# A state-space layer and a gated feed-forward on one core: diagonal matmuls taken out, an inverse root in Newton steps, and the next chunk's input groups moved into the down-projection

## The chip, the cores and the metric

The kernel runs on one core of a Trainium2 chip. TensorE (PE) multiplies matrices into PSUM, VectorE (DVE), ScalarE (ACT) and GpSimd (POOL) work on whole tiles, and SyncE (SP) issues the DMAs. The metric is device time in microseconds (us); lower is better.

## The reference

x is 2048 x 512 in bf16. All matrices are 512 x 512 or, in the feed-forward, 512 x 1376 and 1376 x 512.

```python
xn = _layernorm(x)
dt = exp(log_dt); Lam_bar = exp(dt * Lam); B_bar = ((Lam_bar - 1) / Lam)[:, None] * Bmat
Bu = einsum("bld,pd->blp", xn, B_bar)
h_t = Lam_bar * h_(t-1) + Bu_t                       # over 2048 steps, complex, 512 states
y = 2 * einsum("blp,dp->bld", h, Cmat).real + xn * Dskip
ffn = (silu(xn @ w_gate) * (xn @ w_up)) @ w_down
out = x + y + ffn
```

## The kernel before

The 2048 rows are cut into 4 chunks of 512, each of 4 tiles of 128 rows. Everything stays in SBUF. The complex recurrence is turned by a table of cosines and sines of t times theta into a real scan (decay r), so the steps of a chunk c are:

- **Layer norm.** VectorE takes statistics per tile (L507, L509), adds epsilon (L511, "ve"), GpSimd raises to the power -0.5 (L513, "rstd"). In chunks 0 and 1 VectorE scales (L518); in chunks 2 and 3 it makes a bias (L522, "nmr") and ScalarE scales (L524). The result is xn_sb, which has 8 tile slots.
- **Transpose** of xn into xnT, which has two slots, one for even and one for odd chunks. Chunk 0 uses TensorE (L580) and copies by ScalarE (L586); chunks 1 to 3 use one DMA transpose each (`xt_chunk_dma`, "xTd").
- **FFN groups.** For each of 11 slices of the hidden width one PSUM bank of gate and one of up (L741; chunk 0's first gates in quarters, L768). ScalarE takes silu of the gate (L754, L793, "sg") and copies the up group (L805, "uf", 3 slots); VectorE multiplies them into hT (L807).
- **B groups** ("B c"): 8 PSUM banks of xn times B (L821), copied by ScalarE into u_sb (L828, L830). A copy out of PSUM is called an evacuation below.
- **State steps** on VectorE, for each of 4 slices pt: two products with the tables and a sum (L851, L854, L856: pin1, pin2, v), two scans (L860), two products back (L866, L870: pout1, pout2), a sum into hss (L875), and between chunks some operations on 2 or 4 columns (L873, L882 to L887).
- **Down-projection** `dc_chunk(c)`: "dA" multiplies hT by w_down for 4 tiles (L909, 11 matmuls a tile), "dB" adds hss times the prepared C matrices W12 into the same 4 banks (L925, 8 matmuls a tile). Then VectorE adds the residual while it reads PSUM (L933, L936, "oadd") and a DMA stores the tile.

The term xn * Dskip goes two ways. In chunks 0 and 1 (`rs_dve_from=8`), dA has four more matmuls of 128 x 128 per tile: xnT times diagonal matrices diagD made from Dskip (L912; L498 makes them). In chunks 2 and 3 VectorE multiplies xn by dsk (L596), adds x (L598), and oadd adds that.

W12 needs parameters: cos and sin of theta (L638, L636), then a chain of small products over 128 x 4 (`dve_tt`, L617, and `dve_ts`, L622) to g_re and g_im; then ScalarE scales C (L713, L715) and VectorE finishes (L717, L720). The sine and cosine tables: GpSimd makes t times theta (L692, "tm"), VectorE reduces it into range once for the sine (L694, L696) and once for the cosine (L702, L704), ScalarE takes the sine (L698, L706), GpSimd negates one copy (L700).

**What sets the order.** The kernel records every operation as a task with an engine, a duration that is written by hand (`est`) and what it reads and writes. A planner (`_schedule`) keeps TensorE and SP in the order in which they were recorded. On VectorE, ScalarE and GpSimd it orders the tasks by when they could start and by the longest path behind them. Each engine then runs its list in that order, with semaphore waits, so an instruction that waits holds up all behind it. A DMA transpose waits for all DMAs recorded before it, and a plain DMA waits for the last transpose before it. The order of the program's body before:

```python
        ln_chunk(3)
        dc_chunk(0, mid=lambda: xt_chunk_dma(2))
        u2 = ssm_b_chunk(2)
        ssm_elem_chunk(2, u2)
```

`mid` is called between dA and dB. PSUM has 8 banks; dA holds four until the oadds have read them, and `next_bank` gives the others out in turn.

Of the kernel before, what the change touches and what calls it, by code (L numbers as in the profile page):

```python
# [10 lines left out]
ALU = alu_op_type.AluOpType  # L11
# [13 lines left out]
    rs_dve_from=8,  # L25
# [226 lines left out]
def bass_parallel_sum__ssm_conv_s5__swiglu_ffn__prompt_kernel(  # L252
# [32 lines left out]
    with es:  # L285
# [38 lines left out]
        wtmp = scrC[:, 0:2048].rearrange("p (k d) -> p k d", k=4)  # L324
        vq = sb("vq", [128, NU, 2, 2, CH], B16)
# [8 lines left out]
        praw = sb("praw", [128, 4, PT], B16)  # L334
        prow = sb("prow", [4, 4, 128], B16)
        ecst = sb("ecst", [128, PT], F32)
        diagD = sb("diagD", [128, KT, 128], B16)
# [65 lines left out]
        def dma(name, dst, src, writes, nbytes, reads=(), after=(), out_=False, eng="sp", xpose=False, **kw):  # L403
            after = tuple(after)
            if xpose:
                after = after + tuple(dma_tasks)
                fn = lambda e, dst=dst, src=src: e.dma_start_transpose(out=dst, in_=src)
                est, nb = 2000.0, int(nbytes * 0.8)
            else:
                if xp_state[0] is not None:  # L410
                    after = after + (xp_state[0],)
                fn = lambda e, dst=dst, src=src: e.dma_start(dst, src, **kw)
                est, nb = 330.0 + nbytes / 900.0, nbytes
            t = g.add(eng, fn, reads=reads, writes=writes, name=name, dma=True, after=after, out=out_, est=est, nbytes=nb)
            dma_tasks.append(t)
            if xpose:
                xp_state[0] = t
            return t
# [9 lines left out]
        pload("ld_dskp", 3, A_Dskip)  # L428
# [15 lines left out]

        def loads_stage_b2():
            dma("ld_cre", CT[:, 0], A_C_re, [("CT", 0)], 512 * 512 * 2, xpose=True)
            dma("ld_cim", CT[:, 1], A_C_im, [("CT", 1)], 512 * 512 * 2, xpose=True)
            dma("ld_x8", x_sb[:, 8:12, :], x_v[:, 8:12, :], [("x", a) for a in range(8, 12)], 4 * TILEB)
            dma("ld_wd0", wd[:, 0:FT - 1, :], B_w_down[0:(FT - 1) * 128, :].rearrange("(k p) d -> p k d", p=128), [("wd", 0)], (FT - 1) * 128 * 1024)
            dma("ld_wd1", wd[0:fsz[-1], FT - 1, :], B_w_down[(FT - 1) * 128:Fh, :], [("wd", 1)], fsz[-1] * 1024)  # L450
            dma("ld_x12", x_sb[:, 12:16, :], x_v[:, 12:16, :], [("x", a) for a in range(12, 16)], 4 * TILEB)
            dma("ld_dsk", dsk[:], A_Dskip.partition_broadcast(128), [("dsk",)], 128 * 1024)
# [33 lines left out]
        def params_t(ks):  # L486
            slot = next_tr()

            def tr(e, slot=slot):
                for k in ks:  # L490
                    inst = e.transpose(out=ptr[:, slot, 4 * k:4 * k + 4], in_=prow[0:4, k, :], identity=ident[0:4, 0:4])
                return inst
            g.add("pe", tr, reads=[("prow", k) for k in ks] + [("ident",)], writes=BK(slot), name="parT%d" % ks[0], est=30 * len(ks), ninst=len(ks))
            g.add("dve", lambda e, slot=slot: e.tensor_copy(out=praw[:, ks[0]:ks[-1] + 1].rearrange("p k a -> p (k a)"), in_=ptr[:, slot, 4 * ks[0]:4 * ks[-1] + 4]),
                  reads=BK(slot), writes=[("praw", k) for k in ks], name="parTev%d" % ks[0], est=80, prio=5000.0)
            if 3 in ks:
                for kt in range(KT):
                    g.add("dve", lambda e, kt=kt: e.tensor_scalar(out=diagD[:, kt, :], in0=ident[:], scalar1=praw[:, 3, kt:kt + 1], scalar2=None, op0=ALU.mult),  # L498
                          reads=[("praw", 3), ("ident",)], writes=[("diagD", kt)], name="diagD%d" % kt, est=90)
# [6 lines left out]
        def ln_stats(a, order=False):  # L506
# [9 lines left out]
        def ln_scale(a, norm_act):  # L516
            if not norm_act:
                ln_xn[a] = g.add("dve", lambda e, a=a: e.tensor_scalar(out=xn_sb[:, a % NXN, :], in0=x_sb[:, a, :], scalar1=mv[:, a, 0:1], scalar2=rstd[:, a:a + 1],  # L518
                                                                        op0=ALU.subtract, op1=ALU.mult),
                                  reads=[("x", a), ("mv", a), ("rstd", a)], writes=[("xn", a % NXN)], name="xn%d" % a, est=350)  # L520
            else:
                g.add("dve", lambda e, a=a: e.scalar_tensor_tensor(out=nmr[:, a:a + 1], in0=mv[:, a, 0:1], scalar=-1.0, in1=rstd[:, a:a + 1], op0=ALU.mult, op1=ALU.mult),  # L522
                      reads=[("mv", a), ("rstd", a)], writes=[("nmr", a)], name="nmr%d" % a, est=70)
                g.add("act", lambda e, a=a: e.activation(out=xn_sb[:, a % NXN, :], in_=x_sb[:, a, :], func=AF.Identity, scale=rstd[:, a:a + 1], bias=nmr[:, a:a + 1]),  # L524
                      reads=[("x", a), ("rstd", a), ("nmr", a)], writes=[("xn", a % NXN)], name="xn%d" % a, est=710)

        def ln_tile(a, norm_act):
            ln_stats(a)
            ln_scale(a, norm_act)

        def ln_head():
            for a in range(4):
                ln_stats(a)
            for a in range(4):
                ln_scale(a, False)
            seq = [ln_bn[0], ln_ag[0], ln_ve[0], ln_bn[1], ln_ag[1], ln_xn[0], ln_ve[1], ln_xn[1], ln_bn[2], ln_ag[2], ln_ve[2], ln_bn[3], ln_ag[3], ln_ve[3], ln_xn[2], ln_xn[3]]
            for p, q in zip(seq, seq[1:]):
                if p not in q.deps:
                    q.odeps.add(p)

# [6 lines left out]
        def ln_chunk(c):  # L547
            for a in range(4 * c, 4 * c + 4):
                ln_tile(a, _CFG["ln_norm_act"][c])
# [40 lines left out]
        def xt_chunk_dma(c):  # L590
            s0 = (4 * c) % NXN
            dma("xTd%d" % c, xnT[:, c % 2].rearrange("p j k t -> p (j k) t"), xn_sb[:, s0:s0 + 4, :],
                XNC(c), 4 * TILEB, reads=[("xn", s0 + j) for j in range(4)], xpose=True)

        def resid_tile(a):
            g.add("dve", lambda e, a=a: e.tensor_tensor(out=xn_sb[:, a % NXN, :], in0=xn_sb[:, a % NXN, :], in1=dsk[:], op=ALU.mult),  # L596
                  reads=[("xn", a % NXN), ("dsk",)], writes=[("xn", a % NXN)], name="rs1_%d" % a, est=340)
            g.add("dve", lambda e, a=a: e.tensor_tensor(out=xn_sb[:, a % NXN, :], in0=xn_sb[:, a % NXN, :], in1=x_sb[:, a, :], op=ALU.add),  # L598
                  reads=[("xn", a % NXN), ("x", a)], writes=[("xn", a % NXN)], name="rs2_%d" % a, est=340)
# [15 lines left out]
        def dve_tt(outn, an, bn, op):  # L615
            o, a_, b_ = S(outn), S(an), S(bn)
            small("dve", outn, lambda e: e.tensor_tensor(out=o, in0=a_, in1=b_, op=op), R(an, bn), R(outn))  # L617
# [70 lines left out]
        def _tables():  # L688
            thn = S("thn")
            for pt in range(PT):  # L690
                b = pt % 2
                g.add("pool", lambda e, pt=pt, b=b: e.tensor_scalar(out=tm[:, b, :], in0=iot[:], scalar1=thn[:, pt:pt + 1], scalar2=None, op0=ALU.mult),  # L692
                      reads=R("thn") + [("iot",)], writes=[("tm", b)], name="tm%d" % pt, est=900, prio=_CFG['prio_tab'])
# [6 lines left out]
                g.add("pool", lambda e, pt=pt, b=b: e.tensor_scalar(out=sin2[:, pt, 1, :], in0=sin2[:, pt, 0, :], scalar1=-1.0, scalar2=None, op0=ALU.mult),  # L700
                      reads=[("sinT", pt, 0)], writes=[("sinT", pt, 1)], name="msinT%d" % pt, est=700, prio=_CFG['prio_tab'])
                g.add("dve", lambda e, b=b: e.tensor_scalar(out=tt1[:, b, :], in0=tm[:, b, :], scalar1=0.25, scalar2=MAGIC, op0=ALU.add, op1=ALU.add),  # L702
                      reads=[("tm", b)], writes=[("tt1", b)], name="tt1c%d" % pt, est=400, prio=_CFG['prio_tab'])
                g.add("dve", lambda e, b=b: e.scalar_tensor_tensor(out=tz[:, b, :], in0=tt1[:, b, :], scalar=MAGIC, in1=tm[:, b, :], op0=ALU.subtract, op1=ALU.subtract),  # L704
                      reads=[("tt1", b), ("tm", b)], writes=[("tz", b)], name="tzc%d" % pt, est=660, prio=_CFG['prio_tab'])
                g.add("act", lambda e, pt=pt, b=b: e.activation(out=cosT[:, pt, :], in_=tz[:, b, :], func=AF.Sin, scale=-TWO_PI, bias=halfpi[:, 0:1]),  # L706
                      reads=[("tz", b), ("halfpi",)], writes=[("cosT", pt)], name="cosT%d" % pt, est=700, prio=_CFG['prio_tab'])
# [49 lines left out]
        def ffn_gate_quarters(c, tiles):  # L757
# [21 lines left out]
            params_t([0, 1, 2, 3])  # L779
# [60 lines left out]
        def ssm_elem_chunk(c, units):  # L840
            hb = c % 2
            for (pt, us) in units:
# [16 lines left out]
                for ri in range(2):  # L859
# [3 lines left out]
                        reads=[("v", sl), ("car", c)] + R("r"), writes=[("q", sl, ri)], name="scan%d_%d_%d" % (c, pt, ri), est=1180)  # L863
# [27 lines left out]
        def dc_chunk(c, mid=None, split_last=False):  # L891
# [10 lines left out]
            for (lt, c0, nc_), bk in zip(items, banks):  # L902
                dg = (4 * c + lt < _CFG["rs_dve_from"])
                assert not (dg and nc_ != 512)

                def mmA(e, bk=bk, lt=lt, hb=hb, c=c, c0=c0, nc_=nc_, dg=dg):
# [3 lines left out]
                    if dg:  # L910
                        for kt in range(KT):
                            inst = e.matmul(pbank[:, bk, kt * 128:(kt + 1) * 128], lhsT=xnT[:, c % 2, lt, kt, :], rhs=diagD[:, kt, :], start=False, stop=False)  # L912
                    return inst
                g.add("pe", mmA, reads=[("hT", hb, i) for i in range(FT)] + [("wd", 0), ("wd", 1)] + (XN(c, lt) + [("diagD", kt) for kt in range(KT)] if dg else []),
                      writes=BK(bk), name="mm_dA%d_%d" % (4 * c + lt, c0), est=FT * (216 if nc_ == 512 else 110) + (KT * 60 if dg else 0), ninst=FT + (KT if dg else 0))
            if mid is not None:
                mid()
            for (lt, c0, nc_), bk in zip(items, banks):
# [13 lines left out]
                if a < _CFG["rs_dve_from"]:  # L932
# [111 lines left out]
```

## Time and profile before

| what | value |
|---|---|
| median of 3 runs | 183.66 us (183.64 to 184.3) |
| the profiled execution | 183.74 us |
| its span, first to last instruction | 182.0 us |
| granted TensorE clock in it | 0.999 |
| bytes read and written in HBM | 6.46 MB and 2.10 MB |

The profile comes from one execution. Its table of engines gives the time in which each engine was busy. The chain of work that ended last is followed back from the last instruction: at each step to what released it, or to the instruction before it on its engine; it says which work sets the end. The groups of instructions by line give how many there are, their busy time and the mean duration of one in ns; as instructions overlap a little, the spacing from start to start in the timeline can be shorter. In the groups, after the second bar, stands the idle time of the engine just before them, with what ended it. In the timeline the columns are start, length, engine, line and operation; "SPq" is SyncE's queue that issues DMAs.

### The profile page before, as it was taken

What the parts mean: (1) busy time and instruction counts of PE and PEld (TensorE: products, weight loads), DVE (VectorE), ACT (ScalarE), POOL (GpSimd) and SP (SyncE); (2) the same over time, 40 slices, a digit from 0 to 9 for tenths busy, and PEclk for the clock granted to TensorE, in tenths of its full rate; (3) what the DMA queues carried; (4) which work ended last, traced back from release to release, by engine and by line L of the source; (5) the groups of instructions that cost most, each with busy time, mean ns of one, the idle gap of its engine ahead of it and who ended that gap; (6) DMA issues with size and microseconds to landing.
All of it is one profiled execution on the core that took longest, in us unless ns stands there. A gap on an engine that the chain in (4) does not pass through costs nothing.

```text
span 182.0 us, 2595 instructions
## 1 busy us (share of the span) xinstructions
PE 177.6 (98%) x943; PEld 87.0 (48%) x943; DVE 167.5 (92%) x359; ACT 87.4 (48%) x155; POOL 26.2 (14%) x37
## 2 busy tenths in 40 slices
PE   8899999999999999999999999999999999999994
PEld 3684444444444454444444455444444444444643
DVE  3799889999999998999999999999999999999933
ACT  3249987966798308057766480026667620000000
POOL 3597775000000004000000130000000000000000
PEclk9999999999999999999999999999999999999999
DMA  5993665669400000630000000620000000010202
GB/s 123 318 382 88 117 135 78 120 157 359 131 0 4 0 0 0 122 114 0 0 0 0 0 4 0 115 101 15 0 4 2 0 2 0 0 32 0 86 29 86
DMA packets 23404, 12.39 MB, mean 68 GB/s; under 512 B 15104, under 2 KB 23392, under 8 KB 23392
## 3 DMA queue, kind: packets, MB, share of 16 engines
q1 hardware_dynamic: 23360, 12.23, 25.3%
q8 instruction: 7, 0.11, 0.3%
q14 instruction: 5, 0.04, 0.1%
q10 hardware_dynamic: 32, 0.00, 0.0%
HBM read 6.46 MB, written 2.10 MB: 47 GB/s over the span
## 4 chain that ended last, share of the span: by engine, by line
PE 93%; DVE 3%; DMA 1%; POOL 1%; issue 0%; DVEq 0%
PE pb L741 39%; PE pb L909 21%; PE pb L925 15%; PE pb L821 15%; PE pb L768 1%; DMA x_sb<-in_A_x_dram 1%; DVE st L507 1%; PE pb L912 1%; DVE xn_sb L518 1%; POOL rstd L513 1%; POOL sm L643 1%; DVE mv L509 0%; DVE diagD L498 0%; DVE osb L936 0%; PE pb L580 0%
## 5 line engine op out<-in xcount | busy, mean ns | idle before, releaser
L741 PE MATMUL pb<-xnT,wu 128*128 128x512 bf16 (+1 forms) x176 | 43.7, 379 | 0.0
L909 PE MATMUL pb<-wd,hT 128*128 128x512 bf16 (+3 forms) x187 | 39.7, 367 | 0.0
L860 DVE TENSOR_TENSOR_SCAN vq<-sm,car,vq 128x512 bf16<-128x512 f32 x32 | 39.5, 1269 | 0.1
L741 PE MATMUL pb<-xnT,wg 128*128 128x512 bf16 (+1 forms) x152 | 38.4, 379 | 0.0
L805 ACT ACTIVATE uf<-pb 128x512 bf16<-128x512 f32 (+1 forms) x44 | 26.0, 605 | 16.1 <-DVE hT L807 9.3
L925 PE MATMUL pb<-W,hss 128*128 128x512 bf16 (+1 forms) x136 | 28.3, 366 | 0.0
L821 PE MATMUL pb<-xnT,BT 128*128 128x512 bf16 x128 | 28.1, 379 | 0.0
L741 PEld LDWEIGHTS pb<-xnT,wu 128*128 128x128 bf16 (+1 forms) x176 | 17.6, 100 | 20.1
L909 PEld LDWEIGHTS pb<-wd,hT 128*128 128x128 bf16 (+1 forms) x187 | 18.0, 98 | 18.5
L754 ACT ACTIVATE sg<-pb 128x512 bf16<-128x512 f32 (+1 forms) x38 | 22.6, 606 | 7.1 <-PE pb L741 6.9
L741 PEld LDWEIGHTS pb<-xnT,wg 128*128 128x128 bf16 (+1 forms) x152 | 15.3, 101 | 17.6
L513 POOL TENSOR_TENSOR rstd<-ve,mhalf 128x1 f32<-128x1 f32 x16 | 9.6, 616 | 76.1 <-DVE ve L511 76.1
L925 PEld LDWEIGHTS pb<-W,hss 128*128 128x128 bf16 x136 | 13.2, 98 | 13.9
L821 PEld LDWEIGHTS pb<-xnT,BT 128*128 128x128 bf16 x128 | 12.5, 98 | 15.1
L807 DVE TENSOR_TENSOR hT<-sg,uf 128x512 bf16<-128x512 bf16 (+1 forms) x44 | 18.4, 424 | 1.3 <-ACT uf L805 0.8
L828 ACT ACTIVATE u_sb<-pb 128x512 bf16<-128x512 f32 x16 | 9.5, 596 | 17.2 <-PE pb L821 17.2
L507 DVE BATCH_NORM_STATS2 st<-x_sb 128x6 f32<-128x512 bf16 x16 | 10.2, 683 | 3.0 <-DMA x_sb<-in_A_x_dram 3.0
L830 ACT ACTIVATE u_sb<-pb 128x512 bf16<-128x512 f32 x16 | 9.6, 598 | 3.2 <-PE pb L821 3.2
L866 DVE TENSOR_TENSOR scrA<-vq,cosT 128x1024 bf16<-128x1024 bf16 x16 | 10.9, 684 | 0.0
L870 DVE TENSOR_TENSOR scrA<-vq,sin 128x1024 bf16<-128x1024 bf16 x16 | 10.9, 684 | 0.0
L854 DVE TENSOR_TENSOR scrA<-u_sb,sin 128x1024 bf16<-128x1024 bf16 x16 | 10.9, 682 | 0.0
L851 DVE TENSOR_TENSOR scrA<-u_sb,cosT 128x1024 bf16<-128x1024 bf16 x16 | 10.9, 680 | 0.0
(74 smaller groups left out, 143.2 us busy)
## 6 DMA issues: line engine op xcount, KB each, us to landing
out_dram<-osb SPq DMA_DIRECT2D x15, 128.0 KB, 1.7
x_sb<-in_A_x_dram SPq DMA_DIRECT2D x3, 512.0 KB, 7.5
wd<-in_B_w_down_dram SPq DMA_DIRECT2D x1, 1280.0 KB, 7.1
wg<-in_B_w_gate_dram SPq DMA_DIRECT2D x2, 384.0 KB, 4.6
wu<-in_B_w_up_dram SPq DMA_DIRECT2D x1, 768.0 KB, 6.9
wg<-in_B_w_gate_dram SPq DMA_DIRECT2D x1, 608.0 KB, 7.9
wu<-in_B_w_up_dram SPq DMA_DIRECT2D x1, 608.0 KB, 9.0
x_sb<-in_A_x_dram SPq DMA_DIRECT2D x4, 128.0 KB, 3.0
```

Source lines behind the costliest of these rows:

```text
L507: ln_bn[a] = g.add("dve", lambda e, a=a: e.bn_stats(out=st[:, a, :], in_=x_sb[:, a, :]), reads=[("x", a)], writes=[("st", a)], name="bnst% ...
L513: g.add("pool", lambda e, a=a: e.tensor_tensor(out=rstd[:, a:a + 1], in0=ve[:, a:a + 1], in1=mhalf[:, a:a + 1], op=ALU.pow), reads=[("ve", ...
L741: inst = e.matmul(pbank[0:fs, bk, :].rearrange("p (j t) -> p j t", j=4), lhsT=w[:, kt, i * 128:i * 128 + fs], rhs=xnT[:, c % 2, :, kt, :], ...
L754: g.add("act", lambda e, sl=sl, bk=bk, fs=fs: e.activation(out=sg[0:fs, sl, :], in_=pbank[0:fs, bk, :], func=AF.Silu), reads=BK(bk), write ...
L805: g.add("act", lambda e, ul=ul, bk=bk, fs=fs: e.activation(out=uf[0:fs, ul, :], in_=pbank[0:fs, bk, :], func=AF.Identity), reads=BK(bk), w ...
L807: g.add("dve", lambda e, sl=sl, ul=ul, fs=fs, i=i, hb=hb: e.tensor_tensor(out=hT[0:fs, hb, i, :], in0=sg[0:fs, sl, :], in1=uf[0:fs, ul, :] ...
L821: inst = e.matmul(pbank[:, bk, :].rearrange("p (j t) -> p j t", j=4), lhsT=BT[:, ri, kt, pt * 128:(pt + 1) * 128], rhs=xnT[:, c % 2, :, kt ...
L851: g.add("dve", lambda e, sl=sl, U=U, Cb=Cb: e.tensor_tensor(out=pr2[:, sl, 0], in0=U, in1=Cb, op=ALU.mult), reads=ru + rdt, writes=[("pr", ...
L854: g.add("dve", lambda e, sl=sl, Usw=Usw, S2=S2: e.tensor_tensor(out=pr2[:, sl, 1], in0=Usw, in1=S2, op=ALU.mult), reads=ru + rdt, writes=[ ...
L860: g.add("dve", lambda e, sl=sl, ri=ri, pt=pt, rr=rr, c=c: e.tensor_tensor_scan(out=vq[:, sl, 1, ri, :], data0=rr[:, pt:pt + 1].to_broadcas ...
L909: inst = e.matmul(pbank[:, bk, 0:nc_], lhsT=hT[0:fs, hb, i, lt * 128:(lt + 1) * 128], rhs=wd[0:fs, i, c0:c0 + nc_], start=(i == 0), stop=F ...
L925: inst = e.matmul(pbank[:, bk, 0:nc_], lhsT=hss[:, hb, pt, ri, lt * 128:(lt + 1) * 128], rhs=W12[:, ri, pt, c0:c0 + nc_], start=False, sto ...
```

## The change

1. **No diagonal matmuls.** L912, diagD and the load of Dskip as rows go. All four chunks take the way of VectorE: `resid_chunk` multiplies xn by dsk and adds the product to x_sb in place; every oadd adds x_sb.
2. **Statistics of chunks 2 and 3 on ScalarE**, one pass for the mean and one for the sum of squares per tile, each with an accumulator; then on VectorE, for the four tiles of the chunk together, an inverse root: a first value by integer operations on the bits and four Newton steps, 16 operations on 128 x 4. ScalarE scales as before.
3. **x loaded sooner.** The loads of chunks 2 and 3 of x and of dsk (`loads_x`) are issued before the two C transposes instead of around the load of w_down.
4. **B groups of chunk 2 (3) between dA and dB of chunk 0 (1)**, and the DMA transpose of xn of that chunk recorded before dA.
5. **Parameters and tables.** The 13 small products of `dve_tt` go from VectorE to GpSimd. In the tables, tm and the negated sine go from GpSimd to ScalarE, and the cosine is taken from the absolute value of the sine's reduced argument (a bit mask on VectorE), which takes the place of the second reduction.
6. Some hand-written durations that the planner uses are changed (small products on GpSimd 250 ns, scan 1225, DMA transposes longer), and chunk 2's and 3's transposes have a priority.

```diff
+        def loads_x():
+            dma("ld_x8", x_sb[:, 8:12, :], x_v[:, 8:12, :], [("x", a) for a in range(8, 12)], 4 * TILEB)
+            dma("ld_x12", x_sb[:, 12:16, :], x_v[:, 12:16, :], [("x", a) for a in range(12, 16)], 4 * TILEB)
+            dma("ld_dsk", dsk[:], A_Dskip.partition_broadcast(128), [("dsk",)], 128 * 1024)
...
+        def ln_chunk_act(c):
...
+            for a in A:
+                g.add("act", lambda e, a=a: e.activation(out=junk[:], in_=x_sb[:, a, :], func=AF.Identity, scale=-1.0 / D, accum_out=nmr[:, a:a + 1]),
+                      reads=[("x", a)], writes=[("nmean", a), ("junk",)], name="lsum%d" % a, est=620)
+                g.add("act", lambda e, a=a: e.activation(out=junk[:], in_=x_sb[:, a, :], func=AF.Square, bias=nmr[:, a:a + 1], accum_out=ve[:, a:a + 1]),
+                      reads=[("x", a), ("nmean", a)], writes=[("ss", a), ("junk",)], name="lsq%d" % a, est=710)
...
+            d("lv", lambda e: e.tensor_scalar(out=V, in0=V, scalar1=1.0 / D, scalar2=EPS, op0=ALU.mult, op1=ALU.add), SS, V_)
+            d("li", lambda e: e.tensor_scalar(out=T.bitcast(I32), in0=V.bitcast(I32), scalar1=1, scalar2=None, op0=ALU.logical_shift_right), V_, T_)
+            d("ly", lambda e: e.tensor_scalar(out=Y.bitcast(I32), in0=T.bitcast(I32), scalar1=-1.0, scalar2=1597463007.0, op0=ALU.mult, op1=ALU.add), T_, Y_)
+            for k in range(4):
+                d("na%d" % k, lambda e: e.tensor_tensor(out=T, in0=Y, in1=Y, op=ALU.mult), Y_, T_)
+                d("nb%d" % k, lambda e: e.scalar_tensor_tensor(out=T, in0=T, scalar=-0.5, in1=V, op0=ALU.mult, op1=ALU.mult), T_ + V_, T_)
+                d("nc%d" % k, lambda e: e.scalar_tensor_tensor(out=Y, in0=T, scalar=1.5, in1=Y, op0=ALU.add, op1=ALU.mult), T_ + Y_, Y_)
+            d("nm", lambda e: e.tensor_tensor(out=V, in0=M, in1=Y, op=ALU.mult), NM + Y_, V_)
...
+        def resid_chunk(c):
+            for a in range(4 * c, 4 * c + 4):
+                g.add("dve", lambda e, a=a: e.tensor_tensor(out=xn_sb[:, a % NXN, :], in0=xn_sb[:, a % NXN, :], in1=dsk[:], op=ALU.mult),
...
+                g.add("dve", lambda e, a=a: e.tensor_tensor(out=x_sb[:, a, :], in0=x_sb[:, a, :], in1=xn_sb[:, a % NXN, :], op=ALU.add),
...
-            small("dve", outn, lambda e: e.tensor_tensor(out=o, in0=a_, in1=b_, op=op), R(an, bn), R(outn))
+            small("pool", outn, lambda e: e.tensor_tensor(out=o, in0=a_, in1=b_, op=op), R(an, bn), R(outn), est=250)
...
-                    if dg:
-                        for kt in range(KT):
-                            inst = e.matmul(pbank[:, bk, kt * 128:(kt + 1) * 128], lhsT=xnT[:, c % 2, lt, kt, :], rhs=diagD[:, kt, :], start=False, stop=False)
...
+        resid_chunk(1)
         ln_chunk(3)
-        dc_chunk(0, mid=lambda: xt_chunk_dma(2))
-        u2 = ssm_b_chunk(2)
-        ssm_elem_chunk(2, u2)
+        xt_chunk_dma(2)
+        dc_chunk(0, mid=lambda: units.append(ssm_b_chunk(2)))
+        ssm_elem_chunk(2, units[-1])
```

In the order that the planner gives the changed kernel, cos and sin of theta stand on ScalarE behind the ninth and tenth pair of FFN groups of chunk 1, the last ten small products on GpSimd wait for them, and VectorE's operation between those products (L643, "lm1") stands behind the v of chunk 0's last slice.

## The prediction

> **What bounds the kernel now.** I read the table of engines first, then the chain of work that ended last in order of time, then the timelines of VectorE, ScalarE, GpSimd and the DMA issues.
>
> ```profile
> PE 177.6 (98%) x943; PEld 87.0 (48%) x943; DVE 167.5 (92%) x359; ACT 87.4 (48%) x155; POOL 26.2 (14%) x37
> ```
>
> TensorE is busy 98%, VectorE 92%: two engines are near full, so the chain must say which one sets the end.
>
> ```profile
> 9.68 0.71 DVE xn_sb L518
> 10.39 0.05 issue
> 10.44 0.40 PE pb L580 x4
> ...
> 60.13 2.38 PE pb L909 x11
> 62.51 0.23 PE pb L912 x4
> ...
> 70.54 6.91 PE pb L925 x32
> 77.45 6.91 PE pb L821 x32
> 84.36 18.99 PE pb L741 x88
> ...
> 172.53 6.94 PE pb L925 x40
> ```
>
> The columns are start, length, what. From 10.44 to 179.47 us the chain is TensorE without one wait. So the end moves by what TensorE no longer does, unless a wait appears. The diagonal matmuls (L912, four per tile) are in it: 0.23 eight times.
>
> **What the change takes from the path.** The eight L912 entries are 0.23, 0.23, 0.22, 0.23, 0.23, 0.23, 0.22 and 0.23: **1.82 us**. The head may give a little more. There xn of tile 3 (L518) took 0.79 us beside GpSimd's table multiply (L692 from 9.49), where the one before took 0.40. The multiply goes to ScalarE, so I take 0.40: xn ends at 10.0 instead of 10.39, and TensorE, done with its matmuls at 10.19, wins its idle 0.25. Against that ScalarE now runs a table multiply ahead of the copy of tile 2 out of PSUM: it waits for thn (9.20), takes 0.61 (the spacing of L713), and the copy ends at 10.46 instead of 10.16, so the next matmuls start near 10.52 instead of 10.67. I take **0.15** (between 0 and 0.25). The profiled execution was 183.74 us for a span of 182.0. 183.74 - 1.82 - 0.15 = **181.8**. The median of the runs shown is 183.66, 0.08 lower; that is inside the uncertainty.
>
> **The new TensorE timetable**, from the same lengths: dA of chunk 0 from 60.1 to 69.7, B of chunk 2 to 76.6, dB of chunk 0 to 83.5, FFN 2 to 102.5, dA 1 to 112.0, B 3 to 118.9, dB 1 to 125.8, FFN 3 to 144.8, dA 2 to 154.3, dB 2 to 161.2, dA 3 to 170.8, dB 3 to 177.7. B of chunk 2 is needed 7.8 us sooner than before (77.45), so everything that feeds it is checked. Places in a queue below are those in the changed kernel's instruction order.
>
> **VectorE's work.** Spacings from its timeline:
>
> ```profile
> 79.77 3.63 DVE L860 TENSOR_TENSOR_SCAN vq<-sm,car,vq 128x512 bf16<-128x512 f32 x3
> ...
> 87.51 0.69 DVE L870 TENSOR_TENSOR scrA<-vq,sin 128x1024 bf16<-128x1024 bf16 x1
> 88.11 0.42 DVE L807 TENSOR_TENSOR hT<-sg,uf 128x512 bf16<-128x512 bf16 x1
> 88.44 1.29 DVE L856 TENSOR_TENSOR vq<-scrA 128x1024 bf16<-128x1024 bf16 x2
> ```
>
> Start to start: a scan 1.20, a 1024-wide product 0.60, a 512-wide one 0.33; a small operation 0.07 where free and 0.19 where it needs the one before (L887 at 142.44, the scan behind it 142.63). Removed: statistics of chunks 2 and 3, each 2.9 (64.97 to 67.85) plus four nmr 0.3 and a wait for GpSimd of 0.46, together 7.3; diagD 0.7; thirteen small products 1.5; the second table branch (L702, L704) 5.0. Added: 16 Newton operations per chunk, each needing the one before, 16 x 0.19 = 3.0, twice 6.1; 16 residual operations 5.4; four mask operations at the 0.42 of L694, 1.7. Net -1.3. VectorE's gain is small, and it comes at other places than its load.
>
> The Trainium skill, page "VectorE: DVE Perf Modes", section "Rules for kernel authors", says to minimise the count of operations, which speaks against a chain of small ones. Here the count per chunk is 16 either way, and the rows above already price it.
>
> **What feeds B of chunk 2.** ScalarE's two passes per tile stand between the evacuations of B 0, B 1 and FFN 1, the last behind FFN 1's fifth group. A pass is not in the trace; the nearest row is L524, 0.71 apart; bounds 0.48 (an evacuation) and 1.05 (L524's 0.80 and a second small instruction like L636's 0.25). At 0.7 the last ends near 46.5, at 1.05 some 1 us later. VectorE starts chunk 0's products at 29.6 (B's second group ends at 27.2 + 2 x 0.86, its evacuation takes 0.6) and has until the Newton chain six products, four scans, eight residual operations, six products, two hT products, one v and two casts: 3.6 + 4.8 + 2.7 + 3.6 + 0.7 + 0.6 + 0.15 = 16.2, so it stands there at 45.8. Newton with two hT products between and their waits ends near 50.4 (46.5 + 3.0 + 0.7); the four xn on ScalarE, in turn with FFN 1, near 56; the transpose takes the measured 4.7 and lands near 60.7, needed at 69.7: **9 us to spare**. Its queue:
>
> ```profile
> 24.48 1.77 SPq L407 DMA_TRANSPOSE xnT<-xn_sb  x1
> 29.16 1.30 SPq L407 DMA_TRANSPOSE hss<-in_A_C_re_dram  x1
> 33.97 2.31 SPq L407 DMA_TRANSPOSE hss<-in_A_C_im_dram  x1
> 38.41 0.37 SPq L412 DMA_DIRECT2D x_sb<-in_A_x_dram  x1
> 38.83 1.22 SPq L412 DMA_DIRECT2D wd<-in_B_w_down_dram  x2
> ```
>
> The x loads and dsk (1.15 MB, three issues of 1.75 us together) move in front of the two C transposes, which wait for them: x8 landed 3.6 us after its issue, dsk 7.3 behind 1.4 MB of wd. I take all landed at 35 (bounds 33 and 38.3), C at 45.5, wd at 45.6 + 7.1 = 53, needed at 60.1. **7 us to spare**. dsk is new on VectorE's path: the residual of chunk 0 wants it at 34.4, a wait of 0.6 (bounds 0 and 3.9, in a queue whose next consumer has 9 us).
>
> **Where it is tight: GpSimd's products.** cos and sin of thn, done on ScalarE at 11.84 and 20.77 before, stand now behind FFN 1's evacuations, about 59.0 and 59.8. Then VectorE's lm1 (lam_re - 1) at 60.0 (from 50.4: two scans, five hT products, three h, two pout, two residual operations, three products: 9.5), then seven GpSimd products in a row to g_re, with VectorE waiting for them behind two scans (to 62.6) and ScalarE's W passes waiting for VectorE. Behind those W passes ScalarE has B 2's evacuations. A plain 128x4 product on GpSimd isn't in the trace. Nearest rows:
>
> ```profile
> L513 POOL TENSOR_TENSOR rstd<-ve,mhalf 128x1 f32<-128x1 f32 x16 | 9.6, 616 | 76.1 <-DVE ve L511 76.1
> L650 POOL TENSOR_TENSOR sm<-ecst,sm 128x4 f32<-128x4 f32 x1 | 1.1, 1132 | 0.0
> L454 POOL MEMSET mhalf<- 128x16 f32 x1 | 0.1, 111 | 0.3 <-POOLq L1029 0.3
> ```
>
> A power costs 0.62 for one column and 1.13 for four; a memset 0.11. I take **0.35** a product, nearer the memset since a product has no power series, bounds 0.11 and 1.13, plus 0.05 for the wait. g_re is then at 60.2 + 7 x 0.40 = 63.0. From g_re, VectorE needs 0.3 (factors), 0.6 (pout) and 0.67 (first W), ScalarE then four more W passes and three statistics passes at 0.67 and the first evacuation at 0.5: 6.75 to the end of that. dA of chunk 0 holds four of eight PSUM banks, so B 2 can run four groups (3.46 us) from 69.7 before it needs the first evacuation: 73.1. So g_re may come as late as **66.4**; 3.4 to spare, no stall.
>
> The Trainium skill, "GPSIMD Engine Reference", section "Engine selection", puts elementwise products on VectorE and not on GpSimd. No run here shows one there yet. By its section "Performance versus the Vector engine" (4497 ns for 2048 elements at 2.6 cycles each at 1.2 GHz) the fixed part would be about 0.06 us, an estimate; by it the sum stays 181.8.
>
> **Later stages.** Statistics of chunk 3 feed B 3 at 112.0; xn 12 to 15 end near 80. hss of chunk 1 ends near 106, needed at 118.9. Chunk 3: VectorE's last products of dB 1 come at 125.8 + 0.6, four scans and three hT products bring it to 132.2; there before stood at 129.62 with 36.3 us left to the last hss (165.93); less the three hT products, 132.2 + 35.3 = 167.5, needed at 170.8. **3.3 to spare**, where it was 6.4 (172.4 - 165.9).
>
> **Rivals.**
> 1. *The wait moves to GpSimd's products (ends slower).* At 1.13 a product g_re comes at 60.2 + 7 x 1.18 = 68.5, 2.1 past the limit, and B 2 ends some 2.3 late: 181.8 + 2.3 = 184.1. With VectorE 1 to 3.9 us later than I walk it (dsk, dearer Newton) 185 to 188. It decides from g_re at 66.4, and gives slower from about 68.9. For it: the queue order. Against it: 3.4 us of room. 0.12 for slower, 0.13 for a smaller stall (182.8 to 184.6).
> 2. *VectorE sets the end.* If it loses over 3.3 us that the waits for dB 1 don't absorb, dB 3 waits: 182 to 184, at 1 us each. For it: 92% busy, less room. 0.08.
> 3. *The removed matmuls were hidden*, so nothing changes: 183.7. Against it: they stand in the chain with nothing between. 0.03.
>
> **Numbers.** Forecast 181.2 to 182.7: 0.64. About 0.5% (0.9 us) is what a measurement can tell from no change. Faster by more than that (below 182.8) 0.66, within 0.18, slower 0.16. The range 181.1 to 184.5 takes in the smaller stall and rival 2 and leaves out the worst of rival 1.
>
> **What will show it.** Right: the chain is TensorE alone from about 10.3 to 177.5; no L912; B 2 directly behind dA 0 near 69.6 without idle time; GpSimd's products near 0.35; the last hss before 170. Wrong: TensorE idle between 73 and 80 with ScalarE as releaser (rival 1), or before dB 3 with hss as releaser (rival 2).

## The result, and the profile after

The changed kernel takes **181.74 us** (median of 6 runs, 181.66 to 181.99) against 183.65 for the kernel before (6 runs): a ratio of 0.989, interval [0.9876, 0.9906]. A second measurement of the unedited kernel gave 181.76 (after_again, below). The forecast was 181.8. The profiled execution took 181.75 us for a span of 180.0, at a granted clock of 1.0.

Table of engines, changed kernel:

```profile
PE 175.7 (98%) x910; PEld 85.0 (47%) x910; DVE 164.2 (91%) x354; ACT 101.7 (57%) x195; POOL 12.5 (7%) x34
```

TensorE lost 33 matmul records (32 diagonal ones and a transpose of a parameter) and 1.9 us; VectorE 3.3 us of busy time; GpSimd halved; ScalarE rose by 14 us. Chain that ended last, changed kernel (start, length, what):

```profile
8.98 0.17 DVE sm L666
...
9.17 0.72 ACT scrC L713
9.90 0.49 ACT xnT L606
10.39 0.05 issue
10.44 2.85 PE pb L787 x48
13.29 13.81 PE pb L760 x64
...
59.91 9.51 PE pb L925 x44
69.42 6.91 PE pb L840 x32
76.33 6.91 PE pb L938 x32
83.24 18.99 PE pb L760 x88
...
170.52 6.94 PE pb L938 x40
```

Again TensorE alone, from 10.44 to 177.46. The diagonal groups are gone: dA of chunk 0 lasts 9.51 where it lasted 10.41 (60.13 to 70.54), so 0.90 per chunk and 1.80 in all. B of chunk 2 (L840) follows directly. The first long block starts at 13.29 instead of 13.51, 0.22 sooner; 0.05 of that is x landing sooner (the first statistics start at 2.97 instead of 3.02). In the profiled execution of after_again it starts at 13.45 (statistics at 3.05), so this gain differs by some 0.1 to 0.2 from one execution to another. 1.80 + 0.22 = 2.02, and the profiled executions differ by 183.74 - 181.75 = 1.99.

The head's chain is another one. Before, it went through VectorE's xn of tile 3, 0.71 long. Now that one takes 0.41, and the chain goes through theta (L666), the first table pass on ScalarE (L713) and the copy of tile 2 that stands behind it (L606).

VectorE's last stage is what the chain doesn't show. VectorE's timeline before, from the adds of the last chunk:

```profile
174.36 0.69 DVE L936 TENSOR_TENSOR osb<-pb,xn_sb 128x512 bf16<-128x512 f32 x1 [1.11 <-PE pb L925]
176.09 0.69 DVE L936 TENSOR_TENSOR osb<-pb,xn_sb 128x512 bf16<-128x512 f32 x1 [1.03 <-PE pb L925]
177.82 0.69 DVE L936 TENSOR_TENSOR osb<-pb,xn_sb 128x512 bf16<-128x512 f32 x1 [1.04 <-PE pb L925]
```

and after:

```profile
174.69 0.41 DVE L617 TENSOR_TENSOR xn_sb<-xn_sb,dsk 128x512 bf16<-128x512 bf16 x1
175.14 0.42 DVE L619 TENSOR_TENSOR x_sb<-x_sb,xn_sb 128x512 bf16<-128x512 bf16 x1
175.81 0.69 DVE L945 TENSOR_TENSOR osb<-pb,x_sb 128x512 bf16<-128x512 f32 x1 [0.24 <-PE pb L938]
176.71 0.42 DVE L945 TENSOR_TENSOR osb<-pb,x_sb 128x256 bf16<-128x256 f32 x1 [0.21 <-PE pb L938]
177.55 0.42 DVE L945 TENSOR_TENSOR osb<-pb,x_sb 128x256 bf16<-128x256 f32 x1 [0.42 <-PE pb L938]
```

The bracket is VectorE's wait for TensorE before the instruction. Before, these waits came to 3.8 us over the last stage (1.11 + 1.03 + 1.04, and 0.21 and 0.41 behind them); now to 1.1 (0.21 at 172.34, and the three shown), with residual operations between the last adds. In both kernels VectorE's last add ends 0.5 us after TensorE's last matmul; what has shrunk is the time in which VectorE waits for TensorE before that.

### The profile page after: what moved, and what is told of

Same layout as the page of the kernel before. It is cut to its first block, busy times and chain, and to the rows that moved or that the text cites. A ratio compares the mean times of both kernels' runs of the same rounds, so it can differ in the third digit from the quotient of the medians.

```text
span 180.0 us, 2560 instructions
## 1 busy us (share of the span) xinstructions
PE 175.7 (98%) x910; PEld 85.0 (47%) x910; DVE 164.2 (91%) x354; ACT 101.7 (57%) x195; POOL 12.5 (7%) x34
## 4 chain that ended last, share of the span: by engine, by line
PE 93%; DVE 2%; DMA 1%; POOL 1%; ACT 1%; issue 0%; DVEq 0%
PE pb L760 39%; PE pb L925 21%; PE pb L938 15%; PE pb L840 15%; PE pb L787 2%; DMA x_sb<-in_A_x_dram 1%; DVE st L505 1%; POOL rstd L511 1%; POOL sm L664 1%; ACT scrC L713 0%; DVE xn_sb L515 0%; DVE mv L507 0%; ACT xnT L606 0%; DVE osb L945 0%; DVE ve L509 0%
## 5 line engine op out<-in xcount | busy, mean ns | idle before, releaser
L925 PE MATMUL pb<-wd,hT 128*128 128x512 bf16 (+3 forms) x187 | 38.7, 366 | 0.0
L840 PE MATMUL pb<-xnT,BT 128*128 128x512 bf16 x128 | 28.1, 379 | 0.0
L840 PEld LDWEIGHTS pb<-xnT,BT 128*128 128x128 bf16 x128 | 12.5, 98 | 15.1
L847 ACT ACTIVATE u_sb<-pb 128x512 bf16<-128x512 f32 x16 | 9.5, 596 | 11.1 <-PE pb L840 10.7
L945 DVE TENSOR_TENSOR osb<-pb,x_sb 128x512 bf16<-128x512 f32 (+1 forms) x17 | 11.1, 655 | 1.5 <-PE pb L938 1.3
L875 DVE TENSOR_TENSOR vq<-scrA 128x1024 bf16<-128x1024 bf16 x16 | 10.5, 684 | 0.1
L894 DVE TENSOR_TENSOR hss<-scrA 128x1024 bf16<-128x1024 bf16 x16 | 10.4, 684 | 0.0
```

The source lines that it names most:

```text
L840: inst = e.matmul(pbank[:, bk, :].rearrange("p (j t) -> p j t", j=4), lhsT=BT[:, ri, kt, pt * 128:(pt + 1) * 128], rhs=xnT[:, c % 2, :, kt ...
L925: inst = e.matmul(pbank[:, bk, 0:nc_], lhsT=hT[0:fs, hb, i, lt * 128:(lt + 1) * 128], rhs=wd[0:fs, i, c0:c0 + nc_], start=(i == 0), stop=F ...
L945: g.add("dve", lambda e, bk=bk, a=a, os_=os_, c0=c0, nc_=nc_: e.tensor_tensor(out=osb[:, os_, 0:nc_], in0=pbank[:, bk, 0:nc_], in1=x_sb[:, ...
```

## The experiments

The theory: the time is TensorE's own work plus the head, and every other part of the change only keeps TensorE fed. "VectorE's lag" in the table is the end of its last add minus the end of TensorE's last matmul in the profiled execution; about 0.5 is the least there is, since that add reads the last matmuls. Each ratio is to the kernel before on the same chip, where it took 183.68 (e1, e3, e7, e8), 183.67 (e2, e4_power1, e5, e6) or 183.58 (e4_power1_six, e9, e10, after_again), so a difference of 0.1 between rows can be the chip.

| kernel | median us (runs from, to) | ratio to before | VectorE busy | VectorE's lag |
|---|---|---|---|---|
| before | 183.65 | 1 | 167.5 | 0.51 |
| changed | 181.74 (181.66, 181.99) | 0.989 [0.9876, 0.9906] | 164.2 | 0.52 |
| after_again | 181.76 (181.64, 181.89) | 0.990 [0.9887, 0.9913] | 164.1 | 0.53 |
| e1_residual_only | 185.17 (185.06, 185.21) | 1.008 [1.0065, 1.0090] | 171.4 | 1.66 |
| e2_b_behind | 181.95 (181.75, 182.32) | 0.991 [0.9895, 0.9920] | 163.9 | 0.53 |
| e3_zero_matmuls | 183.43 (183.29, 183.50) | 0.998 [0.9976, 0.9993] | 164.3 | 0.46 |
| e4_power1 | 186.13 (186.08, 186.34) | 1.014 [1.0122, 1.0148] | 163.5 | 0.53 |
| e4_power1_six | 183.12 (182.95, 185.54) | 1.000 [0.9973, 1.0021] | 163.4 | 0.53 |
| e5_stats_vector | 182.11 (181.96, 184.43) | 0.994 [0.9911, 0.9963] | 165.3 | 0.77 |
| e6_x_late | 181.76 (181.59, 182.23) | 0.990 [0.9886, 0.9911] | 164.5 | 0.46 |
| e7_products_vector | 182.01 (181.96, 182.53) | 0.991 [0.9900, 0.9927] | 166.0 | 0.73 |
| e8_copy_first | 181.44 (181.27, 181.54) | 0.987 [0.9861, 0.9888] | 163.2 | 0.45 |
| e9_planner_figures | 184.60 (184.47, 185.02) | 1.006 [1.0046, 1.0070] | 171.4 | 2.31 |
| e10_products_gpsimd | 182.40 (182.30, 182.73) | 0.994 [0.9925, 0.9949] | 166.1 | 0.98 |

### The matmuls put back: e3

```diff
+        zero = sb("zero", [128, 128], B16)
...
+                    if c < 2:
+                        for kt in range(KT):
+                            inst = e.matmul(pbank[:, bk, kt * 128:(kt + 1) * 128], lhsT=ident[:], rhs=zero[:], start=False, stop=False)
```

> The changed kernel with 32 more 128x128 matmuls on constants (identity times zeros, four behind each of the first 8 groups of the down-projection, so the sums are unchanged), where the diagonal ones stood, with no new data to wait for. Theory (each matmul taken from the chain is worth its own time): 8 groups of 0.2275 us come back, 181.74 + 1.82 = 183.56. Rival (the matmuls were hidden beside a wait, and the gain comes from elsewhere): 181.74, and idle time on TensorE before some other group.

183.43, so **1.69 us** come back of the 1.82 expected. Chain of e3, chunk 0's dA:

```profile
59.82 2.32 PE pb L927 x10
62.15 0.23 PE pb L930 x4
...
69.95 0.23 PE pb L930 x4
70.18 6.91 PE pb L842 x32
```

L930 are the matmuls put back, 0.23 for four as L912 had before. dA lasts 70.18 - 59.82 = 10.36, 0.85 more than without, and so does the next one (103.04 to 113.39); there is no wait in it. The rival (the matmuls were hidden) is out: they cost their own time wherever they stand in this chain. The remaining 0.05 a chunk, 0.90 against 0.85, is not explained: these matmuls have other operands.

### One part alone: e1, and what it lacked: e9 and e10

```diff
-    rs_dve_from=8,
+    rs_dve_from=0,
...
-            if 3 in ks:
-                for kt in range(KT):
-                    g.add("dve", lambda e, kt=kt: e.tensor_scalar(out=diagD[:, kt, :], in0=ident[:], scalar1=praw[:, 3, kt:kt + 1], scalar2=None, op0=ALU.mult),
-                          reads=[("praw", 3), ("ident",)], writes=[("diagD", kt)], name="diagD%d" % kt, est=90)
...
+        resid_chunk(0)
...
+        resid_chunk(1)
         ln_chunk(3)
```

> The kernel before with one part of the change alone: no diagonal matmuls, no diagD, the residual of every chunk made on VectorE (8 operations more). Statistics, loads, products and the order of the down-projection stay as they were. Theory (TensorE's own work is the time, and the other parts only keep it fed): 8 groups of 0.2275 us go, and if nothing else becomes late 183.65 - 1.82 = 181.8. But in this kernel's VectorE order the 8 residual operations stand between the statistics of chunk 2 and its normalisation, 8 x 0.34 - 0.7 = 2.0 us, and the transposed x of chunk 2 landed at 76.8 before and would be needed at 76.6: it lands near 78.8, B2 waits about 2.2 us, and the time is near 184.0 (183.3 to 185). Rival (the other parts have no use): 181.8 with B2 directly behind the matmuls ahead of it.

185.17: slower than before by 0.8%, though the diagonal matmuls are gone. VectorE's and TensorE's timelines of e1:

```profile
67.68 1.42 DVE L593 TENSOR_TENSOR xn_sb<-xn_sb,dsk 128x512 bf16<-128x512 bf16 x4
69.02 1.43 DVE L595 TENSOR_TENSOR x_sb<-x_sb,xn_sb 128x512 bf16<-128x512 bf16 x4
70.90 0.16 DVE L518 SCALAR_TENSOR_TENSOR nmr<-mv,rstd 128x1 f32<-128x1 f32 x1 [0.46 <-POOL rstd L509]
...
180.53 0.76 DVE L933 TENSOR_TENSOR osb<-pb,x_sb 128x256 bf16<-128x256 f32 x2
```

```profile
69.40 7.07 PE L922 MATMUL pb<-W,hss 128*128 128x512 bf16 x31
78.34 7.08 PE L818 MATMUL pb<-xnT,BT 128*128 128x512 bf16 x32 [1.88 <-DMA xnT<-xn_sb]
```

The 8 residual operations do stand between statistics and nmr, and TensorE waits 1.88 us for the transpose, as expected (2.2). What the expectation missed is the end: chunk 1's residual is 8 operations more, not counted there, and VectorE ends 1.66 us behind TensorE. That part is rival 2 of the prediction, come true in another kernel. e9 takes B's wait away without touching the work:

```diff
-                est, nb = 2000.0, int(nbytes * 0.8)
+                est, nb = 2000.0, int(nbytes * 1.45)
...
-                XNC(c), 4 * TILEB, reads=[("xn", s0 + j) for j in range(4)], xpose=True)
+                XNC(c), 4 * TILEB, reads=[("xn", s0 + j) for j in range(4)], xpose=True, prio=(1500.0 if c > 1 else 0.0))
```

> The kernel of e1 (the kernel before, its residual made on VectorE for every chunk, no diagonal matmuls) with two of the planner's figures of the changed kernel: a transposing load of x counts 1.45 instead of 0.8 of its bytes, and those of chunks 2 and 3 get a priority of 1500. No instruction is added or removed; in VectorE's order the statistics of chunk 2 move up from behind the first products by the state (row 104) to row 71, ahead of most of it. Theory (of e1's 3.4 us over 181.8, 1.9 was B2's wait for statistics that were placed too late, and 1.3 to 1.5 VectorE's own work, which ends the kernel): B2's wait goes, VectorE still ends last, 183.2 (182.6 to 183.8). Rival (only less work on VectorE makes B2 punctual): 185.2.

184.60. The wait is gone (the matmuls of L818 follow those of L922 at 77.09 without a gap), and yet only 0.57 us were won, where 2.0 were expected. From e9's chain, TensorE's first long block and the end:

```profile
14.19 13.81 PE pb L738 x64
...
169.43 1.20 DVE hss L872 x2
170.63 0.35 DVE xn_sb L593
...
178.41 0.69 DVE osb L933
...
```

The end is VectorE's: TensorE's matmuls ended at 178.37, VectorE's adds at 180.68. So e1's wait for B was in good part hidden beneath VectorE's own work, which sets the end in both. One thing must be taken off: in e9's profiled execution a load of gate weights landed late, and the first long block starts at 14.19, where e1's starts at 13.43. From 26.1 to 79.9 VectorE shows no wait all the same; behind that it waits twice for ScalarE, where e1 does not (0.43 at 79.90 and 0.15 at 91.78). At most these 0.58 us can be the late load's, so of the 1.4 us by which the expected gain was too large, at least 0.8 are VectorE's. Theory and rival of e9's expectation were both wrong in size, and the arithmetic too: it took the 1.3 to 1.5 us beyond B's wait as all that VectorE costs, when it was what VectorE costs *after* TensorE had lost 1.88. e10 takes work off VectorE:

```diff
-        dc_chunk(0, mid=lambda: units.append(ssm_b_chunk(2)))
+        dc_chunk(0)
+        units.append(ssm_b_chunk(2))
...
-                ln_chunk_act(c)
+                for a in range(4 * c, 4 * c + 4):
+                    ln_stats(a)
+                    ln_scale_act(a)
...
-        loads_x()
```

> The changed kernel with three parts undone together: the input groups of chunks 2 and 3 behind the down-projection, statistics and inverse root of chunks 2 and 3 on VectorE and GpSimd, x and D loaded late. What is left of the change is the residual, GpSimd's small products and the planner's figures: beside e9 it is the 13 products that leave VectorE (13 x 0.19 = 2.5 us). Theory (VectorE sets the end once some 1 us more than in the changed kernel is put on it; each of these parts alone cost nothing, and together they use the same slack): TensorE runs without a wait, VectorE ends level with it or up to 0.7 us behind, 182.2 (181.8 to 182.8). Rival (sooner x and ScalarE's statistics are needed as a pair): B2 waits, over 183.5.

182.40, within the expected range, without a wait on TensorE in the down-projection. The expectation names only the products as what leaves VectorE beside e9; the tables' second reduction leaves it too (part 5 of the change is kept whole), and busy time falls by 171.4 - 166.1 = 5.3 us. VectorE's lag is 0.98, half a microsecond over the least.

### Each part undone by itself: e2, e5, e6, e7

e2 is the first hunk of e10's diff, e5 the second, e6 the third (with the loads back at their old places); e7 is

```diff
-            small("pool", outn, lambda e: e.tensor_tensor(out=o, in0=a_, in1=b_, op=op), R(an, bn), R(outn), est=250)
+            small("dve", outn, lambda e: e.tensor_tensor(out=o, in0=a_, in1=b_, op=op), R(an, bn), R(outn))
```

> The changed kernel with the input groups of chunks 2 and 3 behind the whole down-projection of chunks 0 and 1 again, as before, instead of between its two parts; the planner of the kernel may reorder VectorE and ScalarE round it. Theory (the place of these groups only gives VectorE time): in the changed kernel the last W pass ends at 70.7 and the first product by the state at 71.2, and the second part of the down-projection would want them at 69.4. If the planner keeps that pace TensorE waits 1.3 to 1.8 us and the time is 183 to 183.5; if it moves the W passes up by what is not due, 181.7. Rival (the move itself costs or gains time): under 181.5, or with TensorE idle at another place.

> The changed kernel with the statistics and the inverse root of chunks 2 and 3 on VectorE and GpSimd as before (bn_stats, bn_aggr, a power, and -mean x rstd), the normalising pass on ScalarE as it is. Theory (statistics have slack in both forms; VectorE's sum changes by 1 to 2 us and it has 3.7 us to spare at the end): 181.7 within 0.3. Rival (Newton steps on VectorE and sums on ScalarE were needed for the gain): slower by 1 us or more, with TensorE waiting for B2 or for a later product.

> The changed kernel with the last two loads of x and the load of D where they stood in the queue before (round the down-projection's weights). Theory (the sooner load only gives slack: transposed x of chunk 2 is issued at 55.97 and needed at 69.4): the statistics of chunk 2 start near 42 instead of 39, everything of chunk 2 is 2 to 4 us later, and the time is 181.7 within 0.3. Rival (the load is what made room for the statistics on ScalarE): B2 waits, 183 to 186.

> The changed kernel with its 13 small products on VectorE again, as before; nothing else edited. Theory (GpSimd's products are late by nothing that decides): the real factor is ready some 2 us sooner (10 products in a chain at 0.19 to 0.20 instead of 0.45 us: 63.95 - 2.5 = 61.5), VectorE has 2.5 us more work, and the time stays at 181.7 within 0.2. Rival (the products delay B2 as they are): up to 0.5 us faster. Rival (VectorE is short of time): slower by up to 2.5 us.

None of the four moves the median by more than 0.4 us. **e2** 181.95: the planner moves the last W pass up from 69.94 to 67.28, so nothing waits; in its profiled execution the first long block of matmuls began 0.6 us later, behind a weight load that landed late, so the 0.2 is not told from none. **e6** 181.76: the transpose of chunk 2 is issued at 61.53 instead of 55.97, still in time. **e5** 182.11 and **e7** 182.01 put 1.1 and 1.8 us on VectorE, and its lag grows by 0.25 and 0.21: two or three tenths in the end. In e7 the factor is no sooner than on GpSimd (L643 at 64.05 against 63.95), because the planner puts two scans between the products; that point of its expectation fell. VectorE's tail in e7:

```profile
176.35 0.42 DVE L617 TENSOR_TENSOR xn_sb<-xn_sb,dsk 128x512 bf16<-128x512 bf16 x1
176.80 0.42 DVE L619 TENSOR_TENSOR x_sb<-x_sb,xn_sb 128x512 bf16<-128x512 bf16 x1
177.32 0.76 DVE L945 TENSOR_TENSOR osb<-pb,x_sb 128x256 bf16<-128x256 f32 x2
```

No wait is left in front of the last two adds, which ran in one go: the 1.1 us of slack are down to the 0.22 ahead of the add before (175.74). Taken one at a time the parts look useless; together (e10, e9, e1) they are 0.6 to 3.4 us. Some of e5's twelve executions took up to 184.43, and none of those left a trace.

### GpSimd's products: e4

```diff
+        pad = sb("pad", [128, 16, 4], F32)
...
             def fn(e):
+                e.tensor_tensor(out=pad[:, k, 0:1], in0=ecst[:, 0:1], in1=mhalf[:, 0:1], op=ALU.pow)
                 return e.tensor_tensor(out=o, in0=a_, in1=b_, op=op)
```

(in the second kernel only for `k in (5, 6, 7, 9, 10, 11)`)

> The changed kernel with a power of one column (0.55 us in this case's traces), whose result nobody reads, ahead of each of GpSimd's 13 products; orders unchanged. It measures the slack of the products. In the changed kernel the real factor is ready at 63.95; 9 more powers in its way make it 68.9. Theory (from the trace of the changed kernel: ScalarE's last pass for W ends at 68.3 and moves with the factor, the four free banks are full at 72.9 and the first must be read from 72.3 on, so there are 4 us to spare): 68.9 is 1.0 too late, 182.7 (182.2 to 183.4). By the limit that the prediction gave (66.4) it is 2.5 too late, 184.2. Rival (the products decide nothing): 181.7.

> As e4_power1, with the extra power ahead of 6 of the last 10 products instead of all 13. There 10 powers moved the first reading of B2's banks by 4.46 us (70.58 to 75.04), TensorE stood 2.62 us, and then ran at a granted clock of 0.50 to 0.62 for some 3 us, which cost 1.55 more. Theory (the limit lies 1.84 us past the changed kernel's own time, and the lower clock follows only a stand of over 2 us, since e1's stand of 1.88 us left it at 1.0): 6 powers move it by 2.8, TensorE stands 1.0 (0.6 to 1.3), the clock stays 1.0, and the time is 182.75. Rival (the clock falls behind every stand, in proportion): 1.6 us for each us, 183.35.

e4_power1: 186.13, 4.4 us over the changed kernel and 3.4 over the expectation. TensorE's timeline round B of chunk 2:

```profile
69.43 3.62 PE L848 MATMUL pb<-xnT,BT 128*128 128x512 bf16 x16
75.67 5.01 PE L848 MATMUL pb<-xnT,BT 128*128 128x512 bf16 x16 [2.63 <-ACT u_sb L855]
80.52 7.07 PE L946 MATMUL pb<-W,hss 128*128 128x512 bf16 x32
```

Four banks fill, TensorE stands 2.63 us until ScalarE has read the first, and then the other 16 matmuls take 5.01 where the first took 3.62. The table by stretches (PE busy, PEld, VectorE, ScalarE, GpSimd, then the granted clock, DMA share and GB/s) says why:

```profile
73.30:75.50 2.20, 0.00 (x0) 0.00 (x0) 2.20 (x4) 2.14 (x7) 0.00 (x0) 0.91 0.00 0
75.50:78.50 3.00, 2.83 (x7) 1.04 (x8) 3.00 (x10) 3.00 (x9) 0.00 (x0) 0.50 0.00 0
78.50:78.60 0.10, 0.10 (x2) 0.02 (x1) 0.10 (x2) 0.10 (x1) 0.00 (x0) 0.94 0.00 0
78.60:79.00 0.40, 0.40 (x3) 0.18 (x2) 0.40 (x1) 0.40 (x3) 0.00 (x0) 1.00 0.00 0
```

The clock fell to half. At 0.91 over the first 2.2 us it must have been at 0.50 for (1 - 0.91) x 2.2 / 0.5 = 0.4 us of them, so from about 75.1 to 78.5. The expectation's limit was also wrong: it left out the three statistics passes that the planner put on ScalarE between the last W pass and the first reading of B's banks. The prediction had counted them.

e4_power1_six: 183.12, 1.36 over after_again on the same chip (1.0 expected, 1.6 by its rival):

```profile
69.30 3.62 PE L849 MATMUL pb<-xnT,BT 128*128 128x512 bf16 x16
73.87 3.86 PE L849 MATMUL pb<-xnT,BT 128*128 128x512 bf16 x16 [0.95 <-ACT u_sb L856]
```

TensorE stands 0.95 and the clock stays 1.00 throughout. Without the stand the 17th matmul would start 16 x 0.216 = 3.46 behind the first (32 take 6.91), at 72.76; from there the loss is 1.11. The last 12 matmuls wait another 0.22 for the second bank (they start at 74.96, when ScalarE has read it), so 1.33 of the 1.36 is in the trace. One of the twelve executions took 185.54 with a mean granted clock of 0.991, the value of all of e4_power1's, and three more took 183.78 to 184.32 at 1.000. None of these four left a trace: whether a stand of about 1 us lowered the clock in the first, or its stand was longer, stays open.

The two give the limit: the last product ends at 68.50 and at 66.70, TensorE stood 2.63 and 0.95 us, so the factor may come until 68.50 - 2.63 = 65.9 or 66.70 - 0.95 = **65.8** (0.15 less if the stands are counted from start to start). In the changed kernel it comes at 63.9.

### The head: e8, a version that beats both

```diff
         streams = _schedule(g.tasks, engs)
+        acts = streams["act"]
+        i = next(k for k, t in enumerate(acts) if t.name == "xTev2_0")
...
+        acts[i - 1], acts[i] = acts[i], acts[i - 1]
```

> The changed kernel with two neighbours on ScalarE exchanged: the copy of transposed tile 2 out of PSUM goes ahead of the first table pass (L713 at 9.17, 0.72 us), all other orders kept. Theory (the head's remaining wait is that copy, done at 10.39 instead of about 10.0): the copy starts at 9.4 and is done by 10.0, the matmuls of tile 2 start behind the transposes of tile 3 at 10.2 instead of 10.44, and the time is 181.5 (0.2 us less), with the tables 0.6 us later and that hidden. Rival: the time stays, since tile 3's copy, now behind the table pass, is late instead (it starts 10.7 and is needed at 11.65), or since the later tables delay something else.

> The changed kernel itself, unedited, on the chip of these three, so that they have it beside them and e8_copy_first can be set against two measurements of it. Every theory: 181.74 within 0.2.

**181.44**, 0.3 under the changed kernel: its slowest run, 181.54, lies below the fastest of the ten executions of the changed kernel, 181.64. TensorE's timeline of e8:

```profile
9.18 0.39 PE L600 MATMUL pb<-ident,xn_sb 128*128 128x128 bf16 x4
9.40 0.83 PE L787 MATMUL pb<-xnT,wg 128*128 128x128 bf16 x12
10.07 0.39 PE L600 MATMUL pb<-ident,xn_sb 128*128 128x128 bf16 x4
10.29 2.84 PE L787 MATMUL pb<-xnT,wg 128*128 128x128 bf16 x48
```

From the transposes of tile 2 (9.18) to its matmuls (10.29) it is 1.11 us, where the changed kernel has 8.96 to 10.44, 1.48. The matmuls now follow the transposes of tile 3 directly; tile 3's copy starts at 10.71, in time.

## Why the prediction was right

- **The path (1.82).** Measured 1.80 in the chain, and 1.69 come back in e3. Right, and for the reason given.
- **The head (0.15).** 0.22, or 0.17 counted from the first statistics; in after_again 0.06 and 0.09. So 0.15 lies within what the two executions show, and they can't say it more closely. Both halves are in the trace: tile 3's xn at 0.41 (0.40 said) and tile 2's copy late behind the table pass, done at 10.39 (10.46 said). e8 shows what the second one costs: 0.3.
- **What feeds B of chunk 2.** Statistics passes of 0.74 and 0.85 (0.7 was taken), the last done by 46.5 as said; Newton ended at 50.15 (50.4 said, though the terms written there add up to 50.2), ScalarE's xn at 55.8 (56), the transpose was issued at 55.97. The wait for dsk was 0.21 at 35.00 (0.6). Good to half a microsecond; e5 and e6 show that the spare time was real.
- **GpSimd's products.** The group's mean is 0.356 and 0.35 was said, but for another reason than thought: the agreement is luck. GpSimd's timeline, and VectorE's, changed kernel:

```profile
60.16 2.35 POOL L638 TENSOR_TENSOR sm<-sm 128x4 f32<-128x4 f32 x2
```

```profile
60.06 2.46 DVE L879 TENSOR_TENSOR_SCAN vq<-sm,car,vq 128x512 bf16<-128x512 f32 x2
```

  Most products take 0.20 (the median of the 13), and the two that meet VectorE's two scans take as long as a scan, 1.22 at most. So the real factor came at 63.9 instead of 63.0, and the limit lies at 65.8 instead of 66.4 (e4): 1.9 us of room, not 3.4. **The step that was mis-sized is this margin**, by nearly half; the sign held. The limit was late in two terms: from the last product (63.91) to the end of the first reading of a bank (71.16) it is 7.25 and not 6.75, above all since the three statistics passes take 2.30 and not 2.01, and the four banks are full at 72.88 and not at 73.1. Past the limit a microsecond cost 1.4 to 1.7 (1.36 for a stand of 0.95 and the short wait behind it, 4.4 for 2.63 and the lower clock behind it), not the 1.1 that rival 1 was priced at: its case, the factor at 68.5, is e4_power1's, and gave 186.13 instead of 184.1.
- **VectorE's margin (rival 2, 0.08).** The last hss came at 166.86 for 170.52, 3.7 of spare time (3.3 said). But it is not the last thing that VectorE owes: the residual operations of chunks 2 and 3 stand among the last adds, and there the slack is 1.1 us. From there on its work sets the end, though not one for one: 1.8 us more in e7 cost 0.3, 1.9 in e10 0.6, 7.2 in e9 2.9. In e9 4.4 of the 7.2 went into time that VectorE has free in the changed kernel (180.0 - 164.2 = 15.8 there, 182.8 - 171.4 = 11.4 in e9). The prediction's sum for VectorE, -1.3 (-3.3 by busy time, 167.5 to 164.2), was called small and put aside; without the parts that make it negative the same removal is a loss (e1, 185.17). So rival 2 was nearer than the prediction thought. It was avoided by what the change takes off VectorE, and that is the answer to what the other parts were for.

What stays open: the 0.05 us per chunk between e3 and before, the longer executions of e5 and e4_power1_six, and how VectorE's gain divides between the products and the tables, since no run undoes the tables alone.

## What to carry to other kernels

When two engines are at 98% and 91%, work taken off the first and put on the second is worth its time only as far as the second's slack *in its last stage* reaches: read that slack from its waits in front of the last instructions, not from a check halfway. Parts that cost nothing when undone one at a time may share one slack; undo them together before calling them useless. And one instruction that the planner put a place too early in the head (e8) was worth 0.3 us where the whole change was worth 1.9.

## What the runs showed of the hardware

- A small product on GpSimd takes 0.20 us alone and up to 1.22 beside a VectorE scan; a power of one column 0.55 alone and 1.45 (e4_power1, at 61.71) or 1.53 (e4_power1_six, at 60.20) beside one. The Trainium skill, "SBUF — State Buffer", section "Who interferes with whom", says that a VectorE instruction with two inputs in SBUF contends with a GpSimd instruction that reads SBUF, for ports that are an exclusive lock; these rows agree.
- A stand of TensorE of 2.63 us halved the granted clock, from some 2.1 us after the stand began and for 3.4 us; a stand of 1.88 us (e1) and, in the profiled execution, one of 0.95 us left it at 1.00. The Trainium skill, "TensorE: Matmul & The Clock Gate", section "What's actually happening", has two states, half and full, with windows of about 3.4 us that run free: the half clock comes after at least one idle window and the full one after a busy window. The half clock and its length agree; but it came here 2.1 us into a stand, sooner than one idle window, and here the measurement decides.
- A pass of ScalarE with an accumulator is two instructions, 0.62 or 0.72 and then 0.19 for reading the accumulator; start to start the two passes came at 0.74 and 0.85 where nothing stood between (60.49, 61.23, 62.08).
